# Opening two token tiles of a fused attention and SwiGLU kernel: both loaded in float32 by hardware DMA and cast on GpSimd, keys in runs of two tokens, the first block under the common path

## Chip, cores and metric

One core of a Trainium2 chip. The metric is device time in microseconds (us) for one execution of the whole kernel; the median over several executions stands for it. Engines: TensorE (PE, with its weight loads PEld), VectorE (DVE), ScalarE (ACT), GpSimd (POOL), and SyncE (SP), which here only issues DMAs. DMAs issued from SP and ACT have their descriptors made by hardware; those issued from POOL have them made by software on POOL[...].

## What is computed

Causal attention with a window of 64 keys over 8 batches of 576 tokens, 8 heads of 64, and then, over all 4608 tokens, a gated feed-forward block of width 1536:

```python
B, H, S, D = q.shape                       # 8, 8, 576, 64
scores = np.matmul(q, k.transpose(0, 1, 3, 2)) / np.sqrt(D)
rel = pos[:, None] - pos[None, :]
scores = np.where((rel >= 0) & (rel < 64), scores, -1e9)
x = softmax(scores) @ v                    # heads side by side: (4608, 512)
g = x @ w_gate                             # (4608, 1536)
out = (g * sigmoid(g) * (x @ w_val)) @ w_out
```

Inputs and output are float32; the kernel multiplies in bf16.

## The kernel before

The 4608 tokens are cut into nine tiles of 512. A batch has nine blocks of 64 tokens and a tile has eight, so tile t begins with the last t blocks of batch t - 1 and goes on with the first blocks of batch t; `segments(t)` lists the two pieces. For each tile the heads go in four pairs `u`, one head on partitions 0 to 63 and the other on 64 to 127.

**Attention of a tile.** `queries[t]` and `kT[t % 2]` hold q and k transposed (head dimension on partitions). `scores(t, u)` multiplies each block of 64 keys with its own and the next block's queries, ACT takes the exponential into E, and DVE multiplies E by a 0/1 mask. `sums` multiplies E by ones and forms the reciprocal on ACT (Ln, then Exp of the negative). `values` multiplies V with E, and DVE scales the result into `xT[t]`. V is kept twice: in v1 as the tile's tokens lie, 128 to a group, and in v2 displaced by one block of 64, since pairs of key blocks begin at both. `shift_v` fills v2 from v1: three copies, or two for tile 0, done by DMAs on SP in every tile.

**Feed-forward of a tile.** `gate_value(t, m)` makes, for each of 12 slices of 128 columns, g and v (four matmuls each, c = 0 to 3), Silu on ACT and the product hT on DVE. `project(t, s)` multiplies hT with w_out and writes the output rows.

**Order.** The schedule is manual: each engine's and each queue's instructions run in the order in which the program names them, and an instruction that waits holds up all that is behind it on its engine. DMAs are issued under eight counters for hardware and eight for software DMAs; a DMA waits, before it is issued, for the one eight places earlier of its kind.

**The opening (tiles 0 and 1).** Later tiles are transposed by DVE (`turn`); tiles 0 and 1 (`TURNED = 2`) are transposed on TensorE by `transposes(t, u)`, with DVE copies from PSUM to `queries` and to `kT` (L172, L173). Tokens sit four to a partition, so that the transposed keys come out in four groups and the copy to kT (L173) writes with a step of four elements to put them in order. Tile 0 comes as float32: q issued from SP and k from ACT (L79, two heads at a time), then its V from SP (L127). POOL casts q and k by head pair (L345) within `front(0)`. Then POOL issues eight casting loads of tile 1's q and k, casts the V of tile 0 (L139), issues the gate and value weights in four slices of 384 columns (L151), then tile 1's V (L127). SP's queue holds, after V, the shift of tile 0 and the shift of tile 1 (L358).

`front(t, other)` interleaves on PE the transposes of pair u, the scores of pair u - 1, `other`, and the sums of pair u - 2; for tile 1, `other` is `back(0, u)`, the values of tile 0. When `front(1)` is over, the gates of tile 0 start; from m = 7 to 10 the values of tile 1 are put between them (`back(1, m - 7)`).

For tile 0 the first block has no previous keys. There `scores` leaves out j = -1, sets that part of E to zero by a DVE memset (L210), and calls the exponential in four pieces (L212, L215). Tile 1's mask has a part set to zero at L361, where its batch begins.

Of the kernel before, what the change touches and what calls it, by code (L numbers as in the profile page):

```python
# [8 lines left out]
P = 128  # L9
FP32 = mybir.dt.float32  # L10
BF16 = mybir.dt.bfloat16
AF = mybir.ActivationFunctionType
# [5 lines left out]
def kernel(  # L18
# [10 lines left out]
    nc = tc.nc  # L29
    S, D, H = 576, 64, 8  # L30
# [4 lines left out]
    ctx.enter_context(tc.manual_schedule())  # L35
    cst = ctx.enter_context(tc.tile_pool(name="cst", bufs=1))
    stage = ctx.enter_context(tc.tile_pool(name="stage", bufs=2))
    cast = ctx.enter_context(tc.tile_pool(name="cast", bufs=1))
    att = ctx.enter_context(tc.tile_pool(name="att", bufs=2))
    epool = ctx.enter_context(tc.tile_pool(name="epool", bufs=5))  # L40
    fsb = ctx.enter_context(tc.tile_pool(name="fsb", bufs=3))
# [7 lines left out]
    kT = [cst.tile([P, 4, 512], BF16, name=f"kT{i}") for i in range(2)]  # L49
    v1 = [cst.tile([P, 4, H, D], BF16, name=f"v1{i}") for i in range(2)]  # L50
    v2 = [cst.tile([P, 4, H, D], BF16, name=f"v2{i}") for i in range(2)]
    identb = cst.tile([P, P], BF16, name="identb")
    ones = cst.tile([P, D], BF16, name="ones")
    tri = cst.tile([P, 2, 64], BF16, name="tri")
    mask = cst.tile([P, 2, 4, 4, 2, 16], BF16, name="mask")
    maskp = cst.tile([P, 2, 16, 4, 2, 4], BF16, name="maskp")

    def segments(t):

        n0 = 64 * t  # L60
        segs = []
        if n0 > 0:
            segs.append((0, t - 1, S - n0, min(n0, 512)))
        if n0 < 512:
            segs.append((n0, t, 0, 512 - n0))
        return segs

    def blocks(ap, t, lo, hi):

        e = 4 if t < TURNED else 16  # L70
        w = 64 // e
        return ap.rearrange("r (e x) -> r e x", e=e)[:, :, w * lo:w * hi]

    staged, queries, weights, inverse, xT, hT = {}, {}, {}, {}, {}, {}

    def load_runs(eng, dst, src, t, hs):

        for off, b, s0, n in segments(t):
            eng.dma_start(  # L79
                dst[off // 4:(off + n) // 4, hs].rearrange("r h e d -> r h (e d)"),  # L80
                src[b, hs, s0:s0 + n].rearrange("h (r e) d -> r h (e d)", e=4),
            )

    def load_q(t):

# [47 lines left out]
    def stage_v(t):  # L133
        staged[t, "v"] = stage.tile([P, 4, H, D], FP32, name="v_f", tag="v", bufs=1)
        load_v(nc.sync, staged[t, "v"], t)

    def cast_v(t):
        for i in range(4):
            nc.gpsimd.tensor_copy(v1[t % 2][:, i], staged[t, "v"][:, i])  # L139

    def shift_v(t, copy):

        a, b, z = v1[t % 2], v2[t % 2], v1[(t - 1) % 2]
        if t:
            copy(b[64:128, 0], z[64:128, 3])
        copy(b[64:128, 1:4], a[64:128, 0:3])
        copy(b[0:64], a[0:64])

    def weights_gv(f0, f1):
        for src, dst in ((moe_w_gate, wg), (moe_w_val, wv)):  # L150
            nc.gpsimd.dma_start(  # L151
                dst[:, :, f0:f1], src[:, f0:f1].rearrange("(c r) f -> r c f", r=P)
            )
# [7 lines left out]
    def transposes(t, u):  # L161

        tp = ps_f.tile([P, 2, 512], BF16, name="tp", tag="g")
        if u == 0:
            queries[t] = att.tile([P, 4, 512], BF16, name="qT", tag="qT")
        for i, x in enumerate(staged[t]):
            for e in range(4):
                for h in range(2):
                    nc.tensor.transpose(
                        tp[64 * h:64 * h + 64, i, P * e:P * e + P], x[:, 2 * u + h, e, :], identb[:]  # L170
                    )
        nc.vector.tensor_copy(queries[t][:, u, :], tp[:, 0, :])  # L172
        nc.vector.tensor_copy(  # L173
            kT[t % 2][:, u, :].rearrange("p (r e) -> p e r", e=4),
            tp[:, 1, :].rearrange("p (e r) -> p e r", e=4),
        )

    def turn(t, u):
# [13 lines left out]
    def scores(t, u):  # L192

        qT = queries[t][:, u, :]
        E = epool.tile([P, 2, 512], BF16, name="E", tag="E")
        s_ps = ps_a.tile([P, 2, 512], FP32, name="s_ps", tag="a")
        for j in range(-1 if t else 0, 8):
            c = j % 2
            lo, hi = max(0, j), min(8, j + 2)
            src = kT[t % 2] if j >= 0 else kT[(t - 1) % 2]  # L200
            for h in range(2):
                r = slice(64 * h, 64 * h + 64)
                nc.tensor.matmul(  # L203
                    blocks(s_ps[64 * c:64 * c + 64, h], t, lo, hi),
                    src[r, u, 64 * (j % 8):64 * (j % 8) + 64],
                    blocks(qT[r], t, lo, hi),
                )
        Ev, sv = [x[:].rearrange("r h (e x) -> r h e x", e=4) for x in (E, s_ps)]
        if t == 0:
            nc.vector.memset(Ev[64:128, :, :, 0:16], 0.0)  # L210
            for h in range(2):
                nc.scalar.activation(  # L212
                    Ev[0:64, h, :, 0:16], sv[0:64, h, :, 0:16], AF.Exp, scale=0.125
                )
                nc.scalar.activation(  # L215
                    Ev[:, h, :, 16:128], sv[:, h, :, 16:128], AF.Exp, scale=0.125
                )
        else:
            nc.scalar.activation(E[:], s_ps[:], AF.Exp, scale=0.125)  # L219
        nc.vector.tensor_mul(  # L220
            E[:].rearrange("r h x -> r (h x)"),
            E[:].rearrange("r h x -> r (h x)"),
            mask[:].rearrange("r h e i c x -> r (h e i c x)") if t < TURNED
            else maskp[:].rearrange("r h e i c x -> r (h e i c x)"),
        )
        weights[t, u] = E

    def part(ap, t):

        i, c = divmod(t, 2)  # L230
        r = slice(64 - 64 * c, P - 64 * c)
        return ap[r, :, :, i, c, :], tri[r, c, :]
# [36 lines left out]
    def gate_value(t, m):  # L269
        if m == 0:  # L270
            hT[t] = hpool.tile([P, 12, 512], BF16, name="hT", tag="hT")
        g_ps = ps_f.tile([P, 512], FP32, name="g_ps", tag="g")
        v_ps = ps_f.tile([P, 512], FP32, name="v_ps", tag="v")
        for ps, w in ((g_ps, wg), (v_ps, wv)):
            for c in range(4):
                nc.tensor.matmul(  # L276
                    ps[:], w[:, c, P * m:P * m + P], xT[t][:, c, :],
                    start=(c == 0), stop=(c == 3),
                )
        sg = fsb.tile([P, 512], FP32, name="sg", tag="sg")  # L280
        nc.scalar.activation(sg[:], g_ps[:], AF.Silu)  # L281
        nc.vector.tensor_mul(hT[t][:, m, :], sg[:], v_ps[:])  # L282
# [20 lines left out]
    def set_exp():  # L303
        nc.scalar.preload_act_table_set("natural_log_exp_and_others")
# [2 lines left out]
        nc.scalar.preload_act_table_set("silu_and_others")  # L307


    raw = [stage.tile([P, H, 4, D], FP32, name=n, tag=n) for n in "qk"]  # L310
    for u in range(4):
        for eng, dst, src in ((nc.sync, raw[0], q), (nc.scalar, raw[1], k)):
            load_runs(eng, dst, src, 0, slice(2 * u, 2 * u + 2))
    stage_v(0)
    set_exp()
    make_identity(nc, identb[:])
    nc.vector.memset(ones[:], 1.0)
    nc.vector.memset(v2[0][64:128, 0], 0.0)
    nc.gpsimd.memset(tri[:], 1.0)
    for a in range(2):  # L320
        half = tri[64 * a:64 * a + 64]
# [10 lines left out]
            mask[:, 0, :, i], tri[:].rearrange("r c (x e) -> r e c x", e=4)  # L332
        )
    nc.vector.tensor_copy(mask[:, 1], mask[:, 0])

    staged[0] = [cast.tile([P, H, 4, D], BF16, name=n, tag=n) for n in ("q_b", "k_b")]

    def front(t, other=None):

        for u in range(6):  # L340
            if u < 4:
                hs = slice(2 * u, 2 * u + 2)
                if t == 0:
                    for src, dst in zip(raw, staged[0]):
                        nc.gpsimd.tensor_copy(dst[:, hs], src[:, hs])  # L345
                transposes(t, u)
            if 0 < u < 5:
                scores(t, u - 1)
            if other and 0 < u < 5:
                other(u - 1)  # L350
            if u > 1:
                sums(t, u - 2, ps_f.tile([P, 512], FP32, name="d_ps", tag="v"))

    def back(t, u):
        values(t, u, ps_a.tile([P, 2, 512], FP32, name="ao_ps", tag="a")[:, 0])

    def shift_dma(dst, src):
        nc.sync.dma_start(dst, src)  # L358

    front(0)  # L360
    nc.vector.memset(part(mask, 1)[0], 0.0)  # L361
    staged[1] = [
        stage.tile([P, H, 4, D], BF16, name=n + "_n", tag=n) for n in "qk"
    ]
    for half in range(2):
        for dst, src in zip(staged[1], (q, k)):
            load_runs(nc.gpsimd, dst, src, 1, slice(4 * half, 4 * half + 4))
    cast_v(0)
    shift_v(0, shift_dma)
    for s in range(4):  # L370
        weights_gv(384 * s, 384 * s + 384)
    load_v(nc.gpsimd, v1[1], 1)
    shift_v(1, shift_dma)
    front(1, lambda u: back(0, u))
    load_qk(2)
    for c in range(2):
        weights_o(6 * c, 6 * c + 6)
# [1 line left out]
    set_silu()  # L379
    for m in range(12):  # L380
        gate_value(0, m)
        if 7 <= m < 11:
            back(1, m - 7)
    for i in range(4):
# [78 lines left out]
```

The softmax here doesn't subtract the row's maximum and nothing guards it: scores larger than these inputs give would overflow.

## Time and profile before

| what | value |
|---|---|
| median of 13 executions | 350.06 us (349.11 to 353.01) |
| the profiled execution | 350.68 us, its span 349.0 us |
| busy in the span: PE / DVE / ACT / POOL | 325.4 / 210.7 / 163.7 / 142.0 us |
| granted PE clock, mean | 0.976 |
| DMA | 44.36 MB, 78306 packets, mean 127 GB/s |
| first cast of q / first `back(0, u)` on PE / gate matmuls running / first `back(1, u)` | 4.20 / 23.27 / 32.57 / 49.45 us |

The profile comes from one execution with hardware timestamps. In its slices each digit is the busy share of a fortieth of the span in tenths; PEclk is the clock granted to PE, in tenths of full speed. In the timeline each row is start and length in us, engine, source line, operation, output and input, with the idle time before it and what ended that idle time in brackets. SPq and ACTq are the queues that issue DMAs. `<-DMA v<-v` means that the last thing to arrive was a DMA from v to v, here one of the shift copies.

### The profile page before, as it was taken

What the parts mean: (1) busy time and instruction counts of PE and PEld (TensorE: products, weight loads), DVE (VectorE), ACT (ScalarE), POOL (GpSimd) and SP (SyncE); (2) the same over time, 40 slices, a digit from 0 to 9 for tenths busy, and PEclk for the clock granted to TensorE, in tenths of its full rate; (3) what the DMA queues carried; (4) which work ended last, traced back from release to release, by engine and by line L of the source; (5) the groups of instructions that cost most, each with busy time, mean ns of one, the idle gap of its engine ahead of it and who ended that gap; (6) DMA issues with size and microseconds to landing.
All of it is one profiled execution on the core that took longest, in us unless ns stands there. A gap on an engine that the chain in (4) does not pass through costs nothing.

```text
span 349.0 us, 6946 instructions
## 1 busy us (share of the span) xinstructions
PE 325.4 (93%) x2668; PEld 157.5 (45%) x2712; DVE 210.7 (60%) x305; ACT 163.7 (47%) x244; POOL 142.0 (41%) x268
## 2 busy tenths in 40 slices
PE   3567989999999999999999999999999999999994
PEld 2354434444444445444544444445444444454441
DVE  4876336766445775577557755775577557753331
ACT  1849322335343376337633763376337633763310
POOL 6973565757075308650872097408510300000000
PEclk9856999999999999999999999999999999999999
DMA  8999999998589905990599069906990230021013
GB/s 263 191 209 203 183 152 125 181 177 107 146 187 227 185 11 107 234 177 12 107 239 171 14 117 240 156 10 118 238 161 17 77 90 0 18 78 30 2 31 91
DMA packets 78306, 44.36 MB, mean 127 GB/s; under 512 B 58688, under 2 KB 72512, under 8 KB 78272
## 3 DMA queue, kind: packets, MB, share of 16 engines
q0 software_dynamic: 38320, 20.37, 45.3%
q1 hardware_dynamic: 38480, 21.97, 25.1%
q10 hardware_dynamic: 1472, 1.57, 1.5%
q8 instruction: 21, 0.34, 0.4%
q14 instruction: 13, 0.11, 0.1%
HBM read 50.14 MB, written 9.44 MB: 171 GB/s over the span
## 4 chain that ended last, share of the span: by engine, by line
PE 83%; DMA 9%; POOL 4%; issue 1%; ACT 1%; DVE 0%; SPq 0%
PE o_ps L287 26%; PE v_ps L276 25%; PE g_ps L276 25%; DMA wv<-in_moe_w_val_dram 5%; PE ao_ps L258 2%; PE s_ps L203 2%; PE d_ps L245 2%; DMA v<-v 2%; DMA q<-in_q_dram 2%; DMA q_s<-in_q_dram 1%; POOL wg L151 1%; POOL v L139 1%; POOL q_n L79 1%; POOL k_n L79 1%; POOL wv L151 1%
## 5 line engine op out<-in xcount | busy, mean ns | idle before, releaser
L281 ACT ACTIVATE sg<-g_ps 128x512 f32<-128x512 f32 x108 | 64.5, 597 | 121.3 <-PE g_ps L276 93.8
L282 DVE TENSOR_TENSOR hT<-sg,v_ps 128x512 bf16<-128x512 f32 x108 | 74.9, 694 | 71.8 <-PE v_ps L276 70.8
L276 PE MATMUL v_ps<-xT,wv 128*128 128x512 bf16 x425 | 110.8, 381 | 0.4
L276 PE MATMUL g_ps<-xT,wg 128*128 128x512 bf16 x419 | 110.1, 381 | 0.8 <-issue 0.3
L287 PE MATMUL o_ps<-wo,hT 128*128 128x512 bf16 x408 | 96.7, 380 | 1.3 <-issue 0.3
L110 POOL DMA_DIRECT2D k_s<-in_k_dram x124 | 66.2, 542 | 30.8 <-DMA q_s<-in_q_dram 18.5
L276 PEld LDWEIGHTS <-wv 128*128 128x128 bf16 x432 | 42.5, 98 | 51.6 <-issue 1.1
L276 PEld LDWEIGHTS <-wg 128*128 128x128 bf16 x432 | 42.0, 98 | 50.8 <-issue 1.3
L287 PEld LDWEIGHTS <-hT 128*128 128x128 bf16 x432 | 39.7, 98 | 45.1
L263 DVE TENSOR_TENSOR xT<-ao_ps,r 128x512 bf16<-128x512 f32 x36 | 24.8, 690 | 22.4 <-ACT r L249 20.5
L219 ACT ACTIVATE E<-s_ps 128x1024 bf16<-128x1024 f32 x32 | 31.4, 1021 | 14.2 <-PE s_ps L203 14.1
L187 DVE STREAM_TRANSPOSE kT<-k_s 128x512 bf16<-128x512 bf16 x28 | 35.9, 1283 | 0.0
L247 ACT ACTIVATE ld<-d_ps 128x512 f32<-128x512 f32 x36 | 21.3, 591 | 24.9 <-PE d_ps L245 22.7
L240 POOL COPY maskp<-tri 64x64 bf16<-64x64 bf16 x12 | 3.1, 286 | 71.6 <-DVE E L220 71.6
L92 POOL DMA_DIRECT2D q_s<-in_q_dram x52 | 28.9, 564 | 7.4 <-DMA v<-in_v_dram 3.2
L220 DVE TENSOR_TENSOR E<-E,maskp 128x1024 bf16<-128x1024 bf16 x28 | 19.4, 692 | 12.4 <-ACT E L219 12.2
L249 ACT ACTIVATE r<-ld 128x512 f32<-128x512 f32 x36 | 22.7, 630 | 1.2
L183 DVE STREAM_TRANSPOSE qT<-q_s 128x512 bf16<-128x512 bf16 x28 | 19.7, 704 | 0.0
L258 PE MATMUL ao_ps<-E,v 128*64 128x64 bf16 x576 | 15.9, 199 | 4.0 <-DMA v<-v 3.2
L245 PE MATMUL d_ps<-E,ones 128*64 128x512 bf16 x72 | 15.5, 424 | 4.3 <-DVE E L220 3.9
L139 POOL CAST v<-v_f 128x512 bf16<-128x512 f32 x28 | 16.6, 631 | 7.0 <-DMA v_f<-in_v_dram 6.4
L258 PEld LDWEIGHTS <-v 128*64 128x64 bf16 x576 | 14.5, 115 | 9.1 <-DMA v<-v 4.0
(80 smaller groups left out, 151.0 us busy)
## 6 DMA issues: line engine op xcount, KB each, us to landing
v_f<-in_v_dram SPq DMA_DIRECT2D x25, 256.0 KB, 6.6
k_s<-in_k_dram POOLq DMA_DIRECT2D x100, 56.0 KB, 5.5
v<-v SPq DMA_DIRECT2D x9, 256.0 KB, 6.2
v<-v SPq DMA_DIRECT2D x9, 192.0 KB, 5.5
wg<-in_moe_w_gate_dram POOLq DMA_DIRECT2D x4, 384.0 KB, 10.8
wv<-in_moe_w_val_dram POOLq DMA_DIRECT2D x4, 384.0 KB, 12.1
wo<-in_moe_w_out_dram POOLq DMA_DIRECT2D x2, 768.0 KB, 9.7
q_s<-in_q_dram POOLq DMA_DIRECT2D x8, 186.0 KB, 6.2
```

Source lines behind the costliest of these rows:

```text
L92: nc.gpsimd.dma_start(q_s[p0:p0 + n // 16, :, 0:w], q[b, a:H:2, s0:s0 + n].rearrange("u (r e) d -> r u (e d)", e=16) [:, :, 32 * c:32 * c ...
L110: nc.gpsimd.dma_start(k_s[p0:p0 + m // 4, o // P, :, 0:w], k[b, a:H:2, s:s + m].rearrange("u (r e) d -> r u (e d)", e=4) [:, :, 32 * c:32 ...
L187: nc.vector.transpose(kT[t % 2][:, u, :].rearrange("r (g x e) -> r g e x", g=4, e=4), k_s[:, :, u].rearrange("r g (e d) -> r g e d", d=D)[ ...
L219: nc.scalar.activation(E[:], s_ps[:], AF.Exp, scale=0.125)
L245: nc.tensor.matmul(d_ps[64 * h:64 * h + 64, :], ones[:], E[:, h, :])
L249: nc.scalar.activation(r[:], ld[:], AF.Exp, scale=-1.0)
L258: nc.tensor.matmul(blocks(o_ps[64 * h:64 * h + 64], t, m, m + 1), (v1 if m % 2 else v2)[t % 2][:, m // 2, 2 * u + h, :], blocks(E[:, h, :] ...
L263: nc.vector.tensor_mul(xT[t][:, u, :], o_ps[:], inverse.pop((t, u))[:])
L276: nc.tensor.matmul(ps[:], w[:, c, P * m:P * m + P], xT[t][:, c, :], start=(c == 0), stop=(c == 3),)
L281: nc.scalar.activation(sg[:], g_ps[:], AF.Silu)
L282: nc.vector.tensor_mul(hT[t][:, m, :], sg[:], v_ps[:])
L287: nc.tensor.matmul(o_ps[:], hT[t][:, c, P * s:P * s + P], wo[:, c, :], start=(c == 0), stop=(c == 11),)
```

## The change

Both opening tiles are loaded as float32 by hardware DMAs: tile 0's q and V and all of tile 1's q and k from SP, tile 0's k from ACT. Keys now lie two tokens to a partition in two halves of 256 tokens, so that the copy to kT writes with a step of two elements; each pair of tile 0 takes one DMA for q and two for k, each pair of tile 1 five, in the order q, k, q, k, k. POOL casts both tiles by pair inside `front`. The V of tile 0 is cast right after `front(0)`, ahead of tile 1's casts. The first slice of the weights is issued after the cast of tile 1's second pair, the other three after `front(1)`. Tile 0 now takes j = -1 as well, with zeros in kT[1] for the missing keys and a mask part set to zero, which DVE restores between the tiles. The shift of tile 1 is done by three DVE copies after `gate_value(0, 6)`.

```diff
-    cast = ctx.enter_context(tc.tile_pool(name="cast", bufs=1))
+    cast = ctx.enter_context(tc.tile_pool(name="cast", bufs=2))
...
+    def load_pair(t, u):
+        hs = slice(2 * u, 2 * u + 2)
         for off, b, s0, n in segments(t):
+            nc.sync.dma_start(
+                raw[t][0][off // 4:(off + n) // 4, hs].rearrange("r h e d -> r h (e d)"),
+                q[b, hs, s0:s0 + n].rearrange("h (r e) d -> r h (e d)", e=4),
             )
+            o, s, left = off, s0, n
+            while left:
+                m = min(left, 256 - o % 256)
+                x = o % 256 // 2
+                (nc.sync if t else nc.scalar).dma_start(
+                    raw[t][1][x:x + m // 2, hs, o // 256].rearrange("r h e d -> r h (e d)"),
+                    k[b, hs, s:s + m].rearrange("h (r e) d -> r h (e d)", e=2),
+                )
+                o, s, left = o + m, s + m, left - m
+
+    def cast_pair(t, u):
+        hs = slice(2 * u, 2 * u + 2)
+        for src, dst in zip(raw[t], staged[t]):
+            nc.gpsimd.tensor_copy(dst[:, hs], src[:, hs])
...
         nc.vector.tensor_copy(
-            kT[t % 2][:, u, :].rearrange("p (r e) -> p e r", e=4),
-            tp[:, 1, :].rearrange("p (e r) -> p e r", e=4),
+            kT[t % 2][:, u, :].rearrange("p (g r e) -> p g e r", g=2, e=2),
+            tp[:, 1, :].rearrange("p (g e r) -> p g e r", g=2, e=2),
         )
...
-        for j in range(-1 if t else 0, 8):
+        for j in range(-1, 8):
...
-        if t == 0:
-            nc.vector.memset(Ev[64:128, :, :, 0:16], 0.0)
-            for h in range(2):
-                nc.scalar.activation(
...
-        else:
-            nc.scalar.activation(E[:], s_ps[:], AF.Exp, scale=0.125)
+        nc.scalar.activation(E[:], s_ps[:], AF.Exp, scale=0.125)
...
     for u in range(4):
-        for eng, dst, src in ((nc.sync, raw[0], q), (nc.scalar, raw[1], k)):
-            load_runs(eng, dst, src, 0, slice(2 * u, 2 * u + 2))
+        load_pair(0, u)
     stage_v(0)
+    for u in range(4):
+        load_pair(1, u)
...
+    nc.vector.memset(kT[1][:, :, 448:512], 0.0)
...
+    nc.vector.memset(part(mask, 0)[0], 0.0)
...
             if u < 4:
-                hs = slice(2 * u, 2 * u + 2)
-                if t == 0:
-                    for src, dst in zip(raw, staged[0]):
-                        nc.gpsimd.tensor_copy(dst[:, hs], src[:, hs])
+                cast_pair(t, u)
+                if t and u == 1:
+                    weights_gv(0, 384)
                 transposes(t, u)
...
     front(0)
+    dst, src = part(mask, 0)
+    for h in range(2):
+        nc.vector.tensor_copy(dst[:, h], src.rearrange("r (x e) -> r e x", e=4))
     nc.vector.memset(part(mask, 1)[0], 0.0)
-    staged[1] = [
-        stage.tile([P, H, 4, D], BF16, name=n + "_n", tag=n) for n in "qk"
-    ]
-    for half in range(2):
-        for dst, src in zip(staged[1], (q, k)):
-            load_runs(nc.gpsimd, dst, src, 1, slice(4 * half, 4 * half + 4))
     cast_v(0)
     shift_v(0, shift_dma)
-    for s in range(4):
+    front(1, lambda u: back(0, u))
+    for s in range(1, 4):
         weights_gv(384 * s, 384 * s + 384)
     load_v(nc.gpsimd, v1[1], 1)
-    shift_v(1, shift_dma)
-    front(1, lambda u: back(0, u))
     load_qk(2)
...
     for m in range(12):
         gate_value(0, m)
+        if m == 6:
+            shift_v(1, nc.vector.tensor_copy)
         if 7 <= m < 11:
             back(1, m - 7)
```

More of the change, by code (lines that the diff above doesn't have):

```diff
@@ L74 @@
     staged, queries, weights, inverse, xT, hT = {}, {}, {}, {}, {}, {}
-    def load_runs(eng, dst, src, t, hs):
+    def load_pair(t, u):
+        hs = slice(2 * u, 2 * u + 2)
         for off, b, s0, n in segments(t):
-            eng.dma_start(
-                dst[off // 4:(off + n) // 4, hs].rearrange("r h e d -> r h (e d)"),
-                src[b, hs, s0:s0 + n].rearrange("h (r e) d -> r h (e d)", e=4),
-            )
+            nc.sync.dma_start(
+                raw[t][0][off // 4:(off + n) // 4, hs].rearrange("r h e d -> r h (e d)"),
+                q[b, hs, s0:s0 + n].rearrange("h (r e) d -> r h (e d)", e=4),
+            )
+            o, s, left = off, s0, n
[11 more added lines that the diff above has]
+            nc.gpsimd.tensor_copy(dst[:, hs], src[:, hs])
     def load_q(t):
@@ L165, in transposes @@
             queries[t] = att.tile([P, 4, 512], BF16, name="qT", tag="qT")
-        for i, x in enumerate(staged[t]):
+        for i in range(2):
             for e in range(4):
                 for h in range(2):
+                    x = staged[t][i][:, 2 * u + h]
                     nc.tensor.transpose(
-                        tp[64 * h:64 * h + 64, i, P * e:P * e + P], x[:, 2 * u + h, e, :], identb[:]
+                        tp[64 * h:64 * h + 64, i, P * e:P * e + P],
+                        x[:, e, :] if i == 0 else x[:, e // 2, e % 2, :],
+                        identb[:],
                     )
@@ L207, in scores @@
                 )
-        Ev, sv = [x[:].rearrange("r h (e x) -> r h e x", e=4) for x in (E, s_ps)]
-        if t == 0:
-            nc.vector.memset(Ev[64:128, :, :, 0:16], 0.0)
-            for h in range(2):
-                nc.scalar.activation(
[L213 to L217, printed above, removed]
-        else:
-            nc.scalar.activation(E[:], s_ps[:], AF.Exp, scale=0.125)
+        nc.scalar.activation(E[:], s_ps[:], AF.Exp, scale=0.125)
         nc.vector.tensor_mul(
@@ L307, in set_silu @@
         nc.scalar.preload_act_table_set("silu_and_others")
-    raw = [stage.tile([P, H, 4, D], FP32, name=n, tag=n) for n in "qk"]
+    raw = [
+        [
+            stage.tile([P, H, 4, D], FP32, name="q_f", tag="q"),
+            stage.tile([P, H, 2, 2, D], FP32, name="k_f", tag="k"),
+        ]
+        for _ in range(2)
+    ]
+    for t in range(2):
+        staged[t] = [
+            cast.tile([P, H, 4, D], BF16, name="q_b", tag="q_b"),
+            cast.tile([P, H, 2, 2, D], BF16, name="k_b", tag="k_b"),
+        ]
     for u in range(4):
-        for eng, dst, src in ((nc.sync, raw[0], q), (nc.scalar, raw[1], k)):
-            load_runs(eng, dst, src, 0, slice(2 * u, 2 * u + 2))
+        load_pair(0, u)
     stage_v(0)
+    for u in range(4):
+        load_pair(1, u)
     set_exp()
@@ L334 @@
     nc.vector.tensor_copy(mask[:, 1], mask[:, 0])
-    staged[0] = [cast.tile([P, H, 4, D], BF16, name=n, tag=n) for n in ("q_b", "k_b")]
+    nc.vector.memset(part(mask, 0)[0], 0.0)
     def front(t, other=None):
```

## The prediction

> **What bounds the kernel now.** I read the slices of the span first, to find where TensorE is not full.
>
> ```profile
> PE   3567989999999999999999999999999999999994
> PEclk9856999999999999999999999999999999999999
> ```
>
> After the sixth slice (8.7 us each) PE is nearly full; everything the change touches lies ahead of it. So the question is when the first gate matmul starts, and what holes come soon after. Next, PE's own waits in the first 80 us (engine, line, waited for: total us, times, longest).
>
> ```profile
> PE tp L169 <- POOL q_b L345: 5.2, 2, 4.9
> PE d_ps L245 <- DVE E L220: 3.9, 5, 0.9
> PE ao_ps L258 <- DMA v<-v: 3.2, 2, 1.7
> PE s_ps L203 <- DVE kT L173: 2.5, 5, 1.1
> ```
>
> The third row is two stalls on copies that move V from v1 to v2. The chain of waits over the first 56 us shows how each arises (start us, us, what):
>
> ```profile
> 9.61 1.30 POOL q_n L79 x2
> ...
> 14.52 2.74 POOL v L139 x4
> ...
> 22.35 15.72 DMA wv<-in_moe_w_val_dram
> ...
> 42.40 7.00 DMA v<-v
> ...
> 49.45 0.52 PE ao_ps L258 x16
> ```
>
> and the timeline gives the rows around them:
>
> ```profile
> 4.38 5.06 SPq L127 DMA_DIRECT2D v_f<-in_v_dram  x4
> ...
> 9.55 1.35 POOL L79 DMA_DIRECT2D q_n<-in_q_dram  x2
> ...
> 14.51 2.75 POOL L139 CAST v<-v_f 128x512 bf16<-128x512 f32 x4
> ...
> 23.27 0.64 PE L258 MATMUL ao_ps<-E,v 128*64 128x64 bf16 x16 [1.57 <-DMA v<-v]
> ...
> 32.57 1.49 PE L276 MATMUL g_ps<-xT,wg 128*128 128x512 bf16 x3 [0.34 <-issue]
> ...
> 49.45 0.52 PE L258 MATMUL ao_ps<-E,v 128*64 128x64 bf16 x16 [1.65 <-DMA v<-v]
> ```
>
> Read together: POOL issues eight tile-1 loads (9.55 to 14.5), casts V (to 17.3), then SP issues the two tile-0 shift copies at 16.73 and about 17.3; they land 5.6 and 5.9 us later, and PE's `back(0, 0)` starts at 23.27. From there PE, DVE and ACT need 9.3 us until gate matmuls run at 32.57. The second stall, 1.65 us ahead of `back(1, 0)`, is the same kind of copy for tile 1, issued 41.1 to 43.5 after V landed. The end of the kernel follows these two places one for one, because PE is full after them.
>
> **What the Trainium skill says.** *DMA: Bandwidth & Descriptors*, section "Issuing engines are not separate DMA queues": issuing from several engines saves only the sequencer's issue time. Here issue time is what counts: one SP load of 256 KB takes 0.458 us of SP, four span 1.98. *VectorE: DVE Perf Modes*, section "The perf-mode tier table": a bf16 copy within SBUF may run at the 4x rate, 693 ns for 2048 elements, and an operand in PSUM takes that away. The trace agrees as far as it goes: the mask copy of 512 takes 0.294 us, the qT copy from PSUM 0.42. Section "Mode 2x_1P" there wants step 1; kT's copy with its step of four elements takes 1.29 us, slower still than the 0.69 of a one-element-per-cycle operation on 512 elements. *TensorE: Matmul & The Clock Gate*, "Part 1: The HAM clock gate": half clock until some 3.4 us of activity, in a free-running window. The trace agrees: 0.50 in 15 to 25 us, 0.95 by 35 to 40.
>
> **The change, part by part.**
>
> *SP's queue (the step that decides).* The order written for SP becomes: four q, four V, twenty loads for tile 1 (five per head pair), then the two shift copies. Before, the shifts followed V directly and waited only for POOL. The twenty loads also carry waits on the DMA issued eight places earlier.
> - Start of the twenty. V's four issues ended at 9.44 before. Their durations were not those of an issue alone:
>
> ```profile
> L127 SPq DMA_DIRECT2D v_f<-in_v_dram x4: 368/717/2701, 4.4 to 8.6; - x4
> ```
>
>   The 2.70 us one began at 5.84, when the q and k data were still flowing, and ended when the last q had landed (the cast waiting for it started at 8.43). I read this as a full queue, since V comes in 256-byte pieces, 1024 per DMA. That does not go away. Now the first V also waits for q's second load (before: cast at 5.70) instead of k's first (4.35). I take 10.0 for the end of V; the bounds are 7.3 (four plain issues from 5.4) and 12.
> - Twenty issues at 0.495 (1.98/4): 9.9, so SP reaches the shifts at 19.9. Bounds: 0.38 each (a quick output store with its gap), 7.6; 0.6 each, 12.
> - The second shift is issued 0.55 later, 20.45. It lands 5.5 later: between 4.1 and 5.9 in this stretch before; it has the last tile-1 loads ahead of it and weight slice 0 beside it. So **25.95 instead of 23.2, +2.7 us**.
>
> PE stands at `back(0, 0)` meanwhile, with `transposes(1, 2)`, everything later of tile 1, and the gates behind it. The following stretch keeps its length. I walked it with a kT copy of 0.7: ACT sets its end (per head pair E 1.02, ld 0.60, r 0.63), and E of the fourth pair still waits for r of the second. So +2.7 arrives whole at the gates.
>
> *V cast sooner.* cast_v moves ahead of tile 1's front; eight POOL issues (9.55 to 14.51, 5.0 us) leave. V was in at about 12.5 (in that microsecond the DMA rate falls from 254 to 91 GB/s), will be in by 13.5, and is cast by about 15, not 17.3. The 2.3 us are worth nothing, because SP is not there before 19.9.
>
> *Casts on POOL, weights later.* Eight casts at 0.62 are 5.0 us, each behind a load. Pair 1 of tile 1 is loaded near 17 and cast by 18.2, so slice 0 of the weights is issued about when it was (17.2 before), and has some 14 us to land. Slices 1 to 3 come behind pair 3's cast, near 23 instead of 18.7. Before, weight DMAs landed about 2 us apart; so slice 1 is in at 29, slice 3 at 37, where the gates want them at about 40 and 51. Cost zero; the cover is 11 us. Tile 1's V lands by about 42, against `m == 6` near 49. load_qk(2), queued on POOL behind, had landed by the turn at 62.6, and needs a raw buffer that is free from about 10 us on; zero.
>
> *kT copy.* Eight copies go from a step of four elements to two. No row shows this step. Bounds 0.42 (the qT copy) and 1.29 (no gain); I take 0.70, the 512-element rate. The gain of 8 x 0.6 on DVE lies ahead of the shift wait or under ACT; zero.
>
> *First block like the others.* Per pair two more small matmuls (18 take 0.64, 16 took 0.63), one exp of 1.02 for four that spanned 1.19, one memset of 0.11 less. Added on DVE: two memsets (0.11 and up to 0.3), two mask copies (0.15 to 0.3 each) between the tiles. All lie before PE reaches the shift wait, which has some 6 us of room; zero. Loads of k in 512-byte pieces on ACT (eight issues, 0.49 each) may make the first front later by up to 1 us; same cover.
>
> *Tile 1's shift on DVE.* Three copies of 512, 1536 and 2048 elements: 0.29 measured, 0.56 between, 0.69 by the tier table: 1.54, start to start about 1.4. They follow hT of m = 6, which ended 0.94 before PE finished gate 7 (46.86 against 47.80). So `back(1, 0)` starts 0.5 after gate 7 instead of 1.65: **-1.1 us**. hT of m = 7 is queued behind them, 0.5 late, and PE has a second buffer. Bounds: -1.6 (the stall gone) and +1 (POOL issuing descriptors keeps these copies waiting).
>
> *Clock.* Gates start on a slow clock in both; the window's phase may give or take 0.8.
>
> Sum: +2.7 - 1.1 = +1.6. The profiled execution took 350.68 (span 349.0 and 1.7 around it), 0.6 above the median of 350.06. Against it 352.3; against the median **351.7**.
>
> **Rivals.**
> 1. *SP is not held up* (ends on the other side). If the queue is not full at V, as the ACT ring now holds the finer k pieces, and issues take 0.46, SP reaches the shifts at 7.3 + 9.2 = 16.5, as early as before. They land at 22.5, PE gains 0.8 there and 1.1 later: 348.2. Deciding point: shifts issued before about 18. For: q and k issues ran at 0.46. Against: the 2.70 us row. Chance 0.16.
> 2. *SP is held up longer.* Late tile-1 loads share the DMA engines with weight slice 0, k comes in 512-byte pieces, and the waits eight places back bind. Shifts issued at 22.5 to 23, landing at 28.5: +5.3 - 1.1, 354.3. For: V issues elsewhere take up to 5.4 us when POOL's loads are in flight. Against: tile 1's pieces are larger. Chance 0.2.
> 3. *A wash.* The landing shortens to 4.1 as the DMA load of q_n and k_n is gone, and the second stall goes wholly: +1.3 - 1.6, 349.8. Chance 0.16.
>
> My forecast has 0.48; its own range is 350.7 to 353.0.
>
> **How the numbers follow.** A difference under 0.3% (1.05 us) can't be told from none by this measurement. Faster: rival 1, and the low edge of 3: 0.17. Same: most of 3 and the lower part of the forecast: 0.21. Slower: 0.62. Leaving out a tenth at each end, the range is 348.6 to 354.4.
>
> **What would show it.** Right: SP issues shifts at 19 to 21.5, PE's first `ao_ps` waits for v<-v for 5 us or more and starts near 26, gate matmuls run near 35, the wait ahead of `back(1, 0)` is about half a microsecond, kT copies near 0.7. Wrong: shifts issued by 17; PE waiting for casts or weights instead; or DVE copies of over 3 us in all.

## The result, and the profile after

| | before | after |
|---|---|---|
| median | 350.79 us (48 executions) | 355.62 us (11 executions, 353.99 to 357.04) |
| ratio to before | | 1.0133, 95% interval 1.0111 to 1.0156 |
| profiled execution, its span | 350.68, 349.0 us | 356.83, 355.1 us |
| granted PE clock, mean | 0.976 | 0.968 |
| PE busy | 325.4 us | 323.9 us |

The changed kernel is slower by 4.8 us in the medians, three times the forecast 1.6. The traced execution of after lies 1.2 us above the median of its kind, so the traces differ by 6.1 us.

The slices of the span (40 of 8.9 us) of the changed kernel:

```profile
PE   3624799999999999999999999999999999999995
PEclk9955899999999999999999999999999999999998
```

The third and fourth slices, 6 and 7 before, are now 2 and 4; after the sixth PE is nearly full in both. PE's own waits in the first 80 us say which wait it is:

```profile
PE ao_ps L265 <- DMA v<-v: 9.6, 1, 9.6
PE tp L185 <- POOL q_b L97: 5.8, 2, 4.8
...
PE ao_ps L265 <- DVE v L162: 0.8, 1, 0.8
```

The wait for the tile-0 shift was 1.57 us and is 9.6. The one ahead of `back(1, 0)` is now a wait for the third DVE copy (L162), and short. The timeline of SP's queue up to 60 us, with all it issued between V and the shifts (L80 is q, L88 k, L142 V, L376 the shift):

```profile
5.03 5.12 SPq L142 DMA_DIRECT2D v_f<-in_v_dram  x4
10.19 0.82 SPq L80 DMA_DIRECT2D q_f<-in_q_dram  x1
...
11.99 2.71 SPq L88 DMA_DIRECT2D k_f<-in_k_dram  x2
...
21.09 0.96 SPq L88 DMA_DIRECT2D k_f<-in_k_dram  x2
22.16 28.77 SPq L376 DMA_DIRECT2D v<-v  x3
```

V ends at 10.15, the twenty loads fill the time to 22.05, and the shifts come at 22.16 and 22.97 (the last row's length holds a third issue, of tile 2, at 50.5). Two k loads at 11.99 took 2.71 us instead of 0.95. The timeline of all engines:

```profile
20.31 0.90 POOL L166 DMA_DIRECT2D wg<-in_moe_w_gate_dram  x1
...
29.86 0.62 POOL L97 CAST k_b<-k_f 128x512 bf16<-128x512 f32 x1 [4.54 <-DMA k_f<-in_k_dram]
...
31.22 0.64 PE L265 MATMUL ao_ps<-E,v 128*64 128x64 bf16 x16 [9.59 <-DMA v<-v]
...
40.58 1.49 PE L283 MATMUL g_ps<-xT,wg 128*128 128x512 bf16 x3 [0.33 <-issue]
...
55.24 0.69 DVE L162 COPY v<-v 64x2048 bf16<-64x2048 bf16 x1
...
55.98 0.52 PE L265 MATMUL ao_ps<-E,v 128*64 128x64 bf16 x16 [0.76 <-DVE v L162]
```

Stage by stage, from these rows and those of before:

| stage | before | after | difference |
|---|---|---|---|
| start to `back(0, 0)` on PE | 23.27 | 31.22 | +7.95 |
| to the gate matmuls | 9.30 | 9.36 | +0.06 |
| to `back(1, 0)` | 16.88 | 15.40 | -1.48 |
| to the end of the span | 299.55 | 299.12 | -0.43 |

The loss has one place, the first. The third stage gains 0.89 from the wait (1.65 to 0.76) and the rest, about 0.6, from the clock: in the first 3 us of the gates it is granted 0.70 instead of 0.51 (windows of 3 us from the start of the gates), and 0.19 of 3 us is 0.57.

Why a DMA of 256 KB takes 8.2 us there: the DMA view of the stretch from 22.2 to 31.2 us (first the queues with packets, MB and share of the DMA engines' time, then the issues with KB and us to landing):

```profile
q0 software_dynamic: 1056, 0.79, 59.6%
q1 hardware_dynamic: 877, 0.90, 37.2%
...
v<-v SPq DMA_DIRECT2D x1, 256.0 KB, 8.2
v<-v SPq DMA_DIRECT2D x1, 192.0 KB, 8.2
```

Software DMAs take 60% of the DMA engines' time: that is slice 0 of the weights, issued at 20.31 and 21.20, ahead of the shifts. The windows of one microsecond (length, busy shares of PE, PEld, DVE, ACT and POOL with counts, PE clock, DMA share, GB/s) set this against an earlier stretch:

```profile
14.00:15.00 1.00, 0.29 (x2) 0.11 (x2) 0.66 (x1) 0.97 (x3) 0.12 (x1) 1.00 0.08 14
...
27.00:28.00 1.00, 0.00 (x0) 0.00 (x0) 0.00 (x0) 0.00 (x0) 0.00 (x0) 0.50 1.23 238
```

At 14 the DMA engines are all but idle, while one k issue stands on SP from 12.49 to 14.70; at 27 they are full and no compute engine runs. From 14 to 20 their share is 0.51 on the mean, and what SP issues after that goes out together with the weights.

### The profile page after: what moved, and what is told of

It is laid out like the page before. It is cut to its first block, busy times and chain, and to the rows that moved or that the text cites. A ratio compares the mean times of both kernels' runs of the same rounds, so it can differ in the third digit from the quotient of the medians.

```text
span 355.1 us, 6978 instructions
## 1 busy us (share of the span) xinstructions
PE 323.9 (91%) x2676; PEld 156.5 (44%) x2720; DVE 208.0 (59%) x308; ACT 162.6 (46%) x232; POOL 142.8 (40%) x268
## 3 DMA queue, kind: packets, MB, share of 16 engines
q10 hardware_dynamic: 2560, 1.57, 1.6%
## 4 chain that ended last, share of the span: by engine, by line
PE 81%; DMA 10%; SPq 4%; issue 1%; DVE 1%; ACT 1%; ACTq 0%; POOL 0%; POOLq 0%
PE o_ps L294 26%; PE v_ps L283 24%; PE g_ps L283 24%; DMA k_f<-in_k_dram 4%; DMA v<-in_v_dram 3%; PE ao_ps L265 2%; PE s_ps L221 2%; PE d_ps L252 2%; DMA wv<-in_moe_w_val_dram 2%; SPq L88 2%; DMA q_s<-in_q_dram 1%; SPq L80 1%; SPq L142 1%; ACT E L226 1%; ACTq L88 0%
## 5 line engine op out<-in xcount | busy, mean ns | idle before, releaser
L226 ACT ACTIVATE E<-s_ps 128x1024 bf16<-128x1024 f32 x36 | 35.5, 1020 | 24.8 <-PE s_ps L221 24.7
L254 ACT ACTIVATE ld<-d_ps 128x512 f32<-128x512 f32 x36 | 21.3, 591 | 24.3 <-PE d_ps L252 22.2
```

## The experiments

Two accounts of the loss were to be told apart. A: PE waits on the shift copies, which are issued late and land late because slice 0 shares the DMA engines. B: the shift is only one of several late things, and the last loads of tile 1, with the casts behind them, would hold PE up all the same. Edits are against the changed kernel, except where a heading says that the experiment starts from the kernel before. "Landing" is the time from issue to landing of the tile-0 shifts.

### The tile-0 shift by DVE copies

```diff
-    shift_v(0, shift_dma)
+    shift_v(0, nc.vector.tensor_copy)
```

> The changed kernel with tile 0's shift as two DVE copies, as tile 1's is, instead of two DMAs at the end of SP's queue. Theory A (PE's long wait is for the shift DMAs, which stand behind twenty loads on SP and then land slowly): back(0, 0) starts near 22 instead of 31.2; the last cast of tile 1 (29.9 in the changed kernel) is then what the front waits for, gates at about 35.5 instead of 40.6, tile 1's V is then late for the copies at m = 6 (about 2 us); in all about 3 us off the changed kernel, 352.5. Theory B (the loads and casts of tile 1 set the time anyway): back(0, 0) is early, gates stay at 39 to 40.6, under 1 us off.

351.03 us, ratio to before 1.0002 (0.9975 to 1.0028). `back(0, 0)` runs at 20.53 with no wait for V. Next late is the last k load, in the timeline of this kernel:

```profile
25.56 0.61 POOL L97 CAST k_b<-k_f 128x512 bf16<-128x512 f32 x1 [2.42 <-DMA k_f<-in_k_dram]
```

so gates run at 31.48, nine us earlier than in the changed kernel. (This traced execution, at 348.65 us, is among the fastest of its kind; the medians differ by 4.6.) The wait on the shift is the loss, as A says; B's late load is real but was hidden behind it.

### Slice 0 of the weights after front(1)

```diff
-                if t and u == 1:
-                    weights_gv(0, 384)
...
-    for s in range(1, 4):
+    for s in range(4):
```

> The changed kernel with weight slice 0 issued after front(1), with the other three, so that no software DMA is in flight beside the last loads of tile 1 and the shift. Theory A1 (slice 0 holds up the hardware DMAs issued beside it: 8.1 us to land instead of about 4): shifts are still issued at 22.2 and 23, but land within 4 to 5.5, back(0, 0) at 27 to 28.5, last cast of tile 1 near 25, gates near 36.5 to 38, 351.5 to 353. Theory A2 (the place in SP's queue alone): landing still about 8, nothing gained, 355.6.

350.74 us, ratio 0.9989 (0.9966 to 1.0012): this alone, too, takes away the whole loss. SP still reaches the shifts at 21.52. The line of the shift and the timeline of this kernel:

```profile
DMA to landing us min/median/max: 3.7/3.9/4.0
```

```profile
26.24 0.64 PE L265 MATMUL ao_ps<-E,v 128*64 128x64 bf16 x16 [5.06 <-DMA v<-v]
```

With slice 0 out of the way the same DMAs land in 3.9 us instead of 8.2, and the last k is cast at 24.72 instead of 29.86. So slice 0 in flight is what made the landing long. This fits what the Trainium skill says in *DMA: Bandwidth & Descriptors*, section "Issuing engines are not separate DMA queues": DMAs from different engines run on the same 16 DMA engines and interleave. Here that cost the shift 4.3 us.

### The shifts ahead of the loads of pairs 2 and 3

```diff
-    for u in range(4):
+    for u in range(2):
         load_pair(1, u)
...
     shift_v(0, shift_dma)
+    for u in range(2, 4):
+        load_pair(1, u)
```

> The changed kernel with the two shift DMAs put between the loads of tile 1's second and third pair on SP. Theory A (place in the queue): shifts issued near 17.5 and 18, landed by 23.5, back(0, 0) near 23.5; pairs 2 and 3 are issued 1.2 us later and land beside slice 0, last cast at 30 to 31.5, gates at about 36 to 37, V of tile 1 late by 1 to 2 us at m = 6; about 3 us off the changed kernel, 352.5. Theory B (loads and casts set the time): gates at 40 or later.

354.72 us, ratio 1.0105 (1.0068 to 1.0142). The shifts are issued at 16.3 and 16.9, ahead of slice 0, and land in 3.4 to 4.0 us; `back(0, 0)` is at 21.01. But the loads of pair 3 now come behind slice 0:

```profile
30.34 0.61 POOL L97 CAST q_b<-q_f 128x512 bf16<-128x512 f32 x1 [5.15 <-DMA q_f<-in_q_dram]
```

Gates run at 38.11, only 2.5 us before those of the changed kernel, between what A (36 to 37) and B (40 or later) expected; the median is not told apart from the changed kernel's. B's point holds here: whatever SP issues behind slice 0 is late, the shift or the last pair.

### Keys in runs of four, as before

```diff
-            o, s, left = off, s0, n
-            while left:
-                m = min(left, 256 - o % 256)
...
+            (nc.sync if t else nc.scalar).dma_start(
+                raw[t][1][off // 4:(off + n) // 4, hs].rearrange("r h e d -> r h (e d)"),
+                k[b, hs, s0:s0 + n].rearrange("h (r e) d -> r h (e d)", e=4),
+            )
```

> The changed kernel with keys in runs of four tokens again: one DMA for k where there were one or two (tile 0: four on ACT instead of eight, tile 1: sixteen loads on SP instead of twenty), 1024-byte pieces, kT copies with a step of four. Theory A (the count of issues and the full queue on SP decide): shifts issued 2 to 4 us earlier, at 18 to 20, gates 2 to 4 us earlier, 352 to 353.5; kT copies of 1.29 hidden. Theory C (the kT copy on DVE counts): no better than the changed kernel, gates at 40.6 or later.

353.24 us, ratio 1.0054 (1.0034 to 1.0074). SP has sixteen tile-1 loads instead of twenty and ACT half of its k loads. The shifts go out at 18.76, 3.4 us sooner, but slice 0 is issued at 18.19, again ahead of them. The line of the shift in this kernel, and its timeline:

```profile
DMA to landing us min/median/max: 7.6/7.9/8.1
```

```profile
27.56 0.64 PE L260 MATMUL ao_ps<-E,v 128*64 128x64 bf16 x16 [6.73 <-DMA v<-v]
```

The landing is as long as in the changed kernel. The finer keys thus cost 2.4 us in the medians. In these two traces they cost 3.4 us of issue, but 0.75 of that is one issue that stands still in both, for 2.21 us there and 1.46 here. The kT copies are back at 1.29 us each, and yet `back(0, 0)` to gates takes 8.92 us, not longer: the saving on kT was worth nothing here.

### From the kernel before: tile 1's shift alone on DVE

```diff
-    shift_v(1, shift_dma)
...
         gate_value(0, m)
+        if m == 6:
+            shift_v(1, nc.vector.tensor_copy)
```

> The kernel before with one part of the change alone: tile 1's shift as three DVE copies after gate_value(0, 6). Theory: the stall ahead of back(1, 0) falls from 1.65 us to about 0.7, as in the changed kernel (0.76), nothing else moves: 0.9 off, 350.0. Rival (the copies delay hT and the gates behind it by their 1.4 us): no gain or up to 0.5 slower, 350.9 to 351.4.

348.42 us, ratio 0.9934 (0.9911 to 0.9958): some 2 us gained, more than the wait that goes. The timeline of this kernel:

```profile
47.00 0.52 PE L258 MATMUL ao_ps<-E,v 128*64 128x64 bf16 x16 [0.70 <-DVE v L147]
```

`back(1, 0)` is 2.45 us earlier than before, of which the wait explains 0.95. The other 1.5 are an earlier start: in this execution the tile-0 shifts landed in 3.5 to 3.7 us, so that `back(0, 0)` ran at 21.64 and gates at 30.97, and that start was kept. Why they landed sooner is open (see the end of the next part).

### From the kernel before: both shifts on DVE

The edits of the first and the fifth experiment together, on the kernel before.

> The kernel before with both opening tiles' shifts as DVE copies, no other part of the change. Theory: DVE is free between the tiles (17.9 to 19.4), so the copies for tile 0 are done by 19.3 and the wait of 1.57 us ahead of back(0, 0) goes; gates at about 31, back(1, 0) at 47: 2.4 off, 348.5. Rival (DVE is full in the front of tile 1 and hands the 1.2 us on): only the 0.9 of the second stall, 350.

347.89 us, ratio 0.9922 (0.9891 to 0.9952), the lowest median of all, below both kernels, though not told apart from the version with tile 1's shift alone on DVE. `back(0, 0)` at 21.42, gates at 30.76, `back(1, 0)` at 45.47.

### Both remedies in the changed kernel

The tile-0 shift on DVE, and slice 0 after `front(1)`.

> The changed kernel with both remedies: tile 0's shift on DVE and weight slice 0 behind front(1). If what is late next is the software DMA chain on POOL (weights, then tile 1's V, which landed at 49.7 with the second remedy alone), the two gains do not add: gates at 32 to 34 as slice 0 lands, back(1, 0) no earlier than 50.5, time as with either alone, 350 to 351. If the gains add, back(1, 0) comes near 47 and the time is 347.

352.02 us, ratio 1.0027 (1.0006 to 1.0047). Gates run at 31.87, but the gain is given back before `back(1, 0)`. The timeline of this kernel:

```profile
48.96 0.56 DVE L161 COPY v<-v 64x1536 bf16<-64x1536 bf16 x1 [1.68 <-DMA v<-in_v_dram]
...
50.42 0.69 DVE L162 COPY v<-v 64x2048 bf16<-64x2048 bf16 x1 [0.91 <-DMA v<-in_v_dram]
...
51.16 0.51 PE L265 MATMUL ao_ps<-E,v 128*64 128x64 bf16 x16 [3.27 <-DVE v L162]
```

The DVE copies wait for tile 1's V, which is queued on POOL behind all four weight slices and arrives near 50. The two remedies don't add: putting the weights back moves V back as well.

### Keys in runs of four, the tile-0 shift on DVE, slice 0 one pair later

The edits of the first and the fourth experiment, and:

```diff
-                if t and u == 1:
+                if t and u == 2:
                     weights_gv(0, 384)
```

> The changed kernel with tile 0's shift on DVE, keys in runs of four (sixteen loads of tile 1 on SP instead of twenty), and weight slice 0 behind the cast of the third pair instead of the second. If issue count and the collision with slice 0 were what cost time, the last load is issued by 18.2 and landed by 21.5, the last cast is done by 22.5, gates start near 29.5 to 30.5, tile 1's V lands near 44 to 45, back(1, 0) at 46 to 47: 347.5 to 348.5, faster than the kernel before. If the kT copies on DVE or the later weights hold it: gates at 32 or later, 350 and more.

348.73 us, ratio 0.9936 (0.9913 to 0.996). Gates at 31.46, `back(1, 0)` at 47.84 after a wait of 0.71. The changed kernel so mended is faster than before by some 2 us; it is not told apart from the best version.

### From the kernel before: one copy of tile 1's shift on DVE

The first of tile 1's three shift copies (64 KB, from the last group of the tile before) stood in SP's queue right behind tile 0's. It was moved to DVE, to see whether it slows their landing.

```diff
-            copy(b[64:128, 0], z[64:128, 3])
+            (nc.vector.tensor_copy if t == 1 else copy)(b[64:128, 0], z[64:128, 3])
```

> The kernel before with one copy moved: the 64 KB copy of tile 1's shift that follows tile 0's two shift copies on SP at 17.9 is done by DVE; the other two of tile 1 stay DMAs. In the kernel before, tile 0's copies took 5.6 and 5.9 us to land, and 3.5 to 3.7 in the run without tile 1's shift DMAs. If that third copy is what made them slow, they land in about 3.6 again, back(0, 0) at 21.6, the second stall stays at 1.6: about 1.3 off, 349.2. If it was the weights in flight beside them, landing stays near 5.6: 350.5.

350.78 us, ratio 0.9994 (0.9969 to 1.0019). The tile-0 shifts land in 4.0 and 5.3 us, against 4.1 and 5.9 in the kernel before (my expectation has 5.6 there, which is the 64 KB copy's own), so the 64 KB copy alone does not explain the slow landing. But the timeline of this kernel shows something else:

```profile
31.75 0.81 PE L276 MATMUL g_ps<-xT,wg 128*128 128x512 bf16 x3 [0.16 <-issue]
...
49.12 0.52 PE L258 MATMUL ao_ps<-E,v 128*64 128x64 bf16 x16 [3.51 <-DMA v<-v]
```

Gates began 0.82 us earlier than in the kernel before, and `back(1, 0)` only 0.33 earlier than there (49.45), after a wait of 3.51 instead of 1.65 us. With tile 1's shift done by DMA, `back(1, 0)` is pinned by V's arrival (SP issues tile 1's shift from 41.06 on, here, and from 41.09 in the kernel before) and by the copies behind it, which landed 6.0 to 7.0 us after their issue in both traces; most of an earlier start of the gates is given back there.

### From the version with both shifts on DVE: keys in runs of two

Tile 1 still comes by casting DMAs from POOL, ten instead of eight.

> The kernel before with both shifts on DVE, and in addition keys in runs of two tokens (kT copies of 0.72 instead of 1.29), tile 1 still loaded by casting DMAs from POOL, ten issues instead of eight. Without a shift wait the front of tile 1 is paced by DVE and ACT: if DVE's kT copy counts there, gates start 0.5 to 1 us earlier than 30.8, 347.2; if ACT sets the pace as in the walk of the prediction, gates within 0.3 of 30.8, or later by the 1.4 us of the two more issues on POOL: 347.9 to 348.8.

348.54 us, ratio 0.9932 (0.9905 to 0.9958). kT copies take 0.72 us, but tile 0's last k cast moves from 9.31 to 10.41, and V's casts end at 20.2 instead of 18.1. `back(0, 0)` starts at 22.98 (21.42 without), `back(1, 0)` at 47.50 (45.47). In the medians that is 0.65 us more, within the intervals. Finer keys bring nothing even where no shift DMA is waited for.

### The first block as before

The changed kernel with its first block treated as before: j = -1 left out for tile 0, four exponentials and a memset per pair, no mask part to restore.

> The changed kernel with the first block handled as before again: no j = -1 for tile 0, E cleared by DVE, exponential in four pieces, no mask restored. Theory: all of this lies ahead of the wait for the shift DMAs, so back(0, 0) and the gates stay at 31 and 40.5 within a microsecond, 355.6. Rival: the common path's extra work on DVE between the tiles counts, and this is a microsecond faster.

355.73 us, ratio 1.0134 (1.009 to 1.0178), the same as the changed kernel's 355.62: in the medians this part is worth nothing. The traced execution (354.41 us, the fastest of four) has `back(0, 0)` at 30.36 and gates at 39.10, the latter 1.5 us earlier and outside what I expected. Its shifts went out at 21.52 instead of 22.16; so they did with slice 0 after `front(1)`, where the first block is the changed one, so this is no sign of the first block.

## Why the prediction was right or wrong

**Right: direction and place.** The shift DMAs behind tile 1's loads in SP's queue decide; PE waits for `v<-v` "for 5 us or more" (9.6), and the following stretch keeps its length (9.36 for 9.30).

**Right: the issue price and V.** V's issues ended at 10.15, forecast 10.0. Behind the issue that stood still the loads ran at 0.49 us each (five, from 16.19 to 18.64, took 2.45), forecast 0.495.

**Wrong, first term: SP reaches the shifts at 19.9.** It was 22.16. Of the 2.26 us, 0.15 are V's end, 1.75 the one k issue that took 2.21 us (12.49 to 14.70 in the chain of waits), and 0.33 the q issue right behind V, which took 0.82. I counted the full queue for V and not for the loads behind it. What holds that k issue is not shown. V's 256-byte pieces can't have held it to its end, since the casts of V were over at 14.12. The size of the keys' pieces isn't shown to matter either: with the same list of loads the longest k issue took 1.03 us with the tile-0 shift on DVE, 1.30 with both remedies, 1.46 with the shifts moved ahead and 1.55 with slice 0 later, and 1.46 with coarser keys. So part of the 2.21 us belongs to the execution that was traced; with slice 0 later SP was at the shifts at 21.52.

**Wrong, second term: the shift lands 5.5 us after issue.** It took 8.2, and this is the larger error: 2.7 of 5.3 us (0.25 more is the gap between the two issues). I named slice 0 "beside it" and priced the landing from before. I also misread that price: of the 5.6 and 5.9 us that I gave to the two tile-0 copies, the 5.6 is tile 1's 64 KB copy behind them. The DMA view of the kernel before, from 16.7 to 18.1 us:

```profile
v<-v SPq DMA_DIRECT2D x1, 256.0 KB, 5.9
v<-v SPq DMA_DIRECT2D x1, 192.0 KB, 4.1
v<-v SPq DMA_DIRECT2D x1, 64.0 KB, 5.6
```

The 192 KB copy went out there at 16.73, 0.5 us ahead of slice 0 (17.21), and the 256 KB copy at 17.36, 0.15 us after slice 0 had begun. In the changed kernel slice 0 goes out 1.9 us ahead of the first copy and 2.7 ahead of the second. Over the traces: where slice 0 began 0.6 to 2.7 us ahead of a shift copy, the landing was 7.6 to 8.2 us in all three (the changed kernel, keys in runs of four, the first block as before); where it began later, at most 0.2 us ahead, or had been moved away, 3.4 to 5.9 in all five (the kernel before, its two versions with shift DMAs for tile 0, slice 0 after `front(1)`, the shifts moved ahead). Rival 2 said this in words, and with 22.5 to 23 had SP's time nearly right; its 28.5 still allowed 5.5 to 6 us of landing, 2.7 short.

**Wrong, a premise: the end follows both places "one for one".** A later start of the gates does arrive whole, so the miss doesn't come from here. An earlier one doesn't, in the kernel before: the experiment with one copy of tile 1's shift on DVE shows `back(1, 0)` pinned, in one trace. It follows that the two parts of the sum can't always be priced apart: moving tile 1's shift to DVE also lets an earlier start through, which in its traced execution was 1.5 us beside the 0.95 of the wait.

**Right: tile 1's shift on DVE.** Copies of 0.42, 0.54 and 0.69 us, 1.65 from first start to `back(1, 0)` (forecast 1.4), and a wait of 0.76 (forecast 0.5). The stage gained 1.48 for a forecast of 1.1 only because the clock added 0.57, for which I had allowed 0.8 either way; that part is luck. My "the trace agrees" on the clock holds from 15 us on only: in the kernel before it was granted in full up to there, with PE busy for 0.14 us of the first 5.

**Right: the edits costed at zero.** kT at 0.72 (forecast 0.70), V's casts done by 14.1 (by 15), first block nothing. Slices 1 to 3 of the weights were issued from 30.42 on (I had near 23) and the last landed at 46.1 (I had 37), but PE never waited for them. The cover named for slice 0 was for its own landing; what it did to others was not in the sum.

**Sum.** First place +2.7 forecast, +7.95 in the trace; second -1.1, -1.48; the rest 0, -0.37. The trace says +6.1; the medians say +4.8, and the range ended 4.3 above the median that I used (350.06).

**What stays open.** What makes a load's issue on SP stand still for 1.0 to 2.2 us. And why the 256 KB shift copy landed in 5.9 us in the kernel before and in 5.3 with one copy of tile 1's shift on DVE, but in 3.5 with all of tile 1's shift there, while the 192 KB copy ahead of it took 4.1, 4.0 and 3.7. In all three traces slice 0 began 0.1 to 0.2 us ahead of the 256 KB copy; no experiment moves the two against each other that finely.

## What to carry to other kernels

Price a small DMA's landing by what has been issued ahead of it on any queue and is still to be moved, and not by its own landing elsewhere: here one early prefetch of 768 KB cost a 256 KB copy four microseconds on the critical path. Before a gain ahead of a wait is counted, look whether a later wait is pinned by something the change doesn't move. A copy within SBUF that stands behind a long list of loads in an issuing queue can be had from an idle DVE: the two copies of tile 0 took 0.67 and 0.76 us there in the kernel with both shifts on DVE.

## What the hardware showed that I had not expected

- An SP issue of a plain load mostly takes 0.37 to 0.5 us, but one stood for 2.21 us in mid-list. At its end the DMA engines were 0.08 busy (14 to 15), although the loads of 32, 224 and 96 KB issued from 11.05 to 11.99 had yet to land: they took 4.2 to 4.4 us.
- Two shift DMAs of 256 and 192 KB landed in 3.4 to 4.0 us where no software DMA was under way when they were issued (slice 0 after `front(1)`, the shifts moved ahead), and in 7.6 to 8.2 where slice 0, two software DMAs of 384 KB, had begun 0.6 to 2.7 us before them.
- A DVE copy of 512 bf16 from PSUM takes 0.42 us with a step of one element in the output (the qT copy of before), 0.72 with a step of two and 1.29 with a step of four.
